# Attention and gated MLP on one core: the scores and values of two pairs of heads as one group of matmuls each

## The chip, the core and the metric

The kernel runs on one NeuronCore of a Trainium2 chip. Its engines are TensorE (PE, with its weight loads shown apart as PEld), VectorE (DVE), ScalarE (ACT), GpSimd (POOL) and SyncE (SP, which here only issues DMAs). The metric is the device time of one execution in microseconds, lower is better. Matmuls write to PSUM, which has eight banks of 512 fp32 values in each of 128 partitions; everything else works from SBUF.

## What is computed

Eight batches of 576 positions with 8 heads of 64 go through attention with a short causal window, and the concatenated heads through an MLP whose gate is a convolution over the sequence:

```python
scores = scale * np.matmul(q, k.transpose(0, 1, 3, 2))
rel = pos[:, None] - pos[None, :]
mask_plain = (rel >= 0) & (rel < 32)                          # heads 0 to 3
mask_dil = (rel >= 0) & (rel < 128) & (rel % 4 == 0)          # heads 4 to 7
attn = softmax(np.where(masks, scores, -1e9))
x = np.matmul(attn, v).transpose(0, 2, 1, 3).reshape(B, S, H * D)      # 8 x 576 x 512
h = np.maximum(x @ w_in, 0.0)                                 # 512 -> 1024
conv_out = sum of conv_w[k] * (h shifted by k - 1), k = 0, 1, 2
out = h * sigmoid(conv_out) @ w_out                           # 1024 -> 512
```

w_in, w_out and conv_w arrive as 64-bit floating-point numbers, as pairs of 32-bit words.

## The kernel before

**Attention.** A batch has four pairs of heads p = 0 to 3: two plain ones (kind 0) and two dilated ones (kind 1). `attention(b, p)` adds the tasks of one pair. A query block has 32 rows and sees 64 keys, so a head has 18 blocks; `scores()` (L250, matmul on L258) computes the 36 blocks of a pair with matmuls on 64x32 tiles of the array into the PSUM tile `att`, into nine slots of 64 columns: blocks 0 to 15 fill the two banks of the two heads, the leftovers 16 and 17 go to a third bank, on two of the four groups of 32 partitions for each head. In dilated pairs a leftover takes two matmuls. The softmax follows on DVE and ACT: scores plus mask out of `att` (L270, two additions), row maximum (L272), exponential, row sum, reciprocal (L292), product (L293), transposition in blocks of 32 into `pt` (L295). In batches 0 and 1 (`SLOTS`) the exponential is nine ACT instructions with their sums (L279); later it is one, with one more DVE pass ahead (L285) and one behind (L290). `values()` (L306) multiplies by `v` with matmuls on 32x64 tiles, into `att` again: 40 (plain) or 32 (dilated) in the main part, 8 or 16 for the leftovers. Its result is split into a rounded part `x..a` (ACT, L344) and the remainder `x..b`: in batches 0 and 1 (`HELPED`) by PE, which subtracts `x..a` in place with matmuls by minus one (L351, L354), and an ACT cast (L359); later by DVE (L361).

**The MLP.** `expert(b)`: the first layer computes 8 chunks of 128 columns in two halves of 288 positions. A half takes 12 matmuls 128x288 (L386): for each of the four pairs' `x`, high times high, high times low, low times high. ACT's ReLU writes `h` (L393). The gate of a chunk: a scaled copy (ACT, L404), two convolution taps (DVE, L398), sigmoid (ACT, L409), the product with `h` (DVE, L411), then high and low part into `g` (ACT L413, DVE L415). The second layer takes 24 matmuls of 512 columns (L431) for each 128 positions, 256 columns in batch 0; ACT copies them out (L441) and SP stores them.

**Weights.** The eight chunks of w_in and w_out are converted on the chip into a high and a low part by `weights()` (L495 to L510: two ACT and seven DVE instructions of 1024 columns).

**Order.** Nothing is issued as written. Each operation is a task with an engine, a guessed cost, a due time and the buffers it needs. `Planner.order()` imitates the engines with these costs and takes, among the tasks of an engine that could start within 0.25 us of the first, the one with the smallest due time; the `DUE` table holds the due times. The resulting order of each engine is the program. A task waits in the plan until a buffer of its pool is free. The pools that matter here: one `att` tile of four PSUM banks for scores and values alike, two `qk`, three `v`, three `s`, two `pt`, seven `x`, three `h`, three `c`, two `mm` and two `nn` banks for the two layers, two `out`.

## Time and profile before

| | |
|---|---|
| median of 3 runs | 533.38 us (532.96 to 534.69) |
| the profiled execution | 535.56 us, its span 533.8 us |
| L431, second layer, PE | 960 matmuls, 212.0 us |
| L386, first layer, PE | 1536 matmuls |
| L306, values, PE | 3072 matmuls, 44.7 us |
| L258, scores, PE | 2432 matmuls, 36.6 us |
| DVE, ACT busy | 397.3 us, 303.7 us |

The span is the time from the first to the last instruction of the program; the execution's own time is 1.8 us longer. The trace counts each fp32 matmul of the scores and values twice (1216 and 1536 in the program). A matmul's duration overlaps those of its neighbours, so what one costs is read from the distance of starts.

### The profile page before, as it was taken

The numbers are of one execution on the slowest core, as the hardware profiler recorded it, in microseconds if no ns is written. First come the engines' busy times: TensorE is split into PE (matmuls) and PEld (weight loads), VectorE is DVE, ScalarE is ACT, GpSimd is POOL, SyncE is SP. The second block draws the span as 40 slices with busy tenths as digits, with TensorE's granted clock in tenths as the row PEclk, the third lists the DMA queues.
The fourth block names the chain that finished last, engine by engine and source line by source line (L and its number), as shares of the span: only waits on it lengthen the run. The fifth ranks groups of instructions, "written<-read, shape, count | busy, mean of one in ns | idle before, by whom it ended". The sixth has DMA issues, their size and how long they took to land.

```text
span 533.8 us, 17819 instructions
## 1 busy us (share of the span) xinstructions
PE 505.9 (95%) x8048; PEld 449.4 (84%) x8048; DVE 397.3 (74%) x611; ACT 303.7 (57%) x660; POOL 1.0 (0%) x15
## 2 busy tenths in 40 slices
PE   3569999999999999999999999999999999999996
PEld 2459899998877998789977899789988899789985
DVE  5987999998986799859996569828997277607900
ACT  4975998638632587237742377517764386427710
POOL 0000000000000000000000000000000000000000
PEclk9999999999999999999999999999999999999999
DMA  8846721233145312451224401321313100110011
GB/s 301 297 164 210 241 60 31 80 127 101 43 170 163 97 32 79 154 182 59 83 67 149 148 33 48 121 96 53 104 47 119 52 2 1 59 42 1 0 50 50
DMA packets 16556, 52.24 MB, mean 98 GB/s; under 512 B 2016, under 2 KB 3168, under 8 KB 15456
## 3 DMA queue, kind: packets, MB, share of 16 engines
q1 hardware_dynamic: 16336, 51.02, 28.6%
q8 instruction: 63, 1.03, 0.8%
q14 instruction: 13, 0.11, 0.1%
q10 hardware_dynamic: 144, 0.08, 0.1%
HBM read 41.66 MB, written 9.44 MB: 96 GB/s over the span
## 4 chain that ended last, share of the span: by engine, by line
PE 80%; DVE 8%; ACT 7%; DMA 3%; issue 1%; ACTq 0%
PE nn L431 34%; PE mm L386 31%; PE att L306 8%; PE att L258 4%; ACT s L279 3%; PE nn L386 2%; DVE c L398 2%; PE att L351 1%; DMA qk<-in_qk_p_dram 1%; DVE t L501 1%; DVE wo L510 1%; ACT c L409 1%; DMA c<-in_mask_dram 1%; DVE c L411 1%; DVE g L415 1%
## 5 line engine op out<-in xcount | busy, mean ns | idle before, releaser
L431 PE MATMUL nn<-wo,g 128*128 128x512 f32 (+1 forms) x960 | 212.0, 375 | 0.0
L431 PEld LDWEIGHTS nn<-wo,g 128*128 128x128 f32 x960 | 163.4, 188 | 33.4
L398 DVE SCALAR_TENSOR_TENSOR c<-h,conv_sb,c 128x576 f32<-128x576 f32 x128 | 103.5, 816 | 32.8 <-ACT c L404 31.1
L393 ACT ACTIVATE h<-mm 128x288 f32<-128x288 f32 x120 | 48.5, 408 | 43.9 <-PE mm L386 40.8
L441 ACT COPY out<-nn 128x512 f32<-128x512 f32 (+1 forms) x40 | 21.7, 542 | 72.5 <-PE nn L431 45.1
L413 ACT CAST g<-c 128x576 fp32r<-128x576 f32 x64 | 42.4, 672 | 17.7 <-DVE c L411 15.7
L411 DVE TENSOR_TENSOR c<-c,h 128x576 f32<-128x576 f32 x64 | 47.9, 756 | 5.9 <-ACT c L409 5.4
L306 PEld LDWEIGHTS att<-pt,v 32*64 32x64 f32 x3072 | 41.2, 140 | 13.1 <-issue 8.5
L415 DVE TENSOR_TENSOR g<-c,g 128x576 fp32r<-128x576 f32 x64 | 47.6, 755 | 4.5 <-ACT g L413 3.4
L404 ACT ACTIVATE c<-h,conv_sb 128x576 f32<-128x576 f32 x64 | 49.4, 778 | 1.3
L386 PE MATMUL mm<-x1a,wi 128*128 128x288 f32 x176 | 49.7, 297 | 0.0
L258 PE MATMUL att<-qk 64*32 64x64 f32 x2432 | 36.6, 237 | 13.4 <-DMA qk<-in_qk_p_dram 5.3
L258 PEld LDWEIGHTS att<-qk 64*32 64x32 f32 x2432 | 30.4, 112 | 22.2 <-issue 7.7
L409 ACT ACTIVATE c<-c 128x576 f32<-128x576 f32 x64 | 43.2, 684 | 10.3 <-DVE c L398 9.4
L306 PE MATMUL att<-pt,v 32*64 32x64 f32 (+2 forms) x3072 | 44.7, 234 | 3.8 <-DVE s L270 1.3
L386 PE MATMUL mm<-x2a,wi 128*128 128x288 f32 x144 | 41.6, 304 | 1.3 <-ACT h L393 1.3
L386 PE MATMUL mm<-x0a,wi 128*128 128x288 f32 x144 | 40.6, 297 | 0.0
L270 DVE TENSOR_TENSOR s<-att,mask_sb 128x512 f32<-128x512 f32 x64 | 26.6, 450 | 16.3 <-PE att L258 16.2
L386 PE MATMUL mm<-x6a,wi 128*128 128x288 f32 x128 | 36.6, 301 | 0.8 <-ACT h L393 0.7
L386 PE MATMUL mm<-x5a,wi 128*128 128x288 f32 x128 | 36.2, 298 | 0.2 <-ACT h L393 0.2
L386 PE MATMUL mm<-x4a,wi 128*128 128x288 f32 x128 | 35.9, 295 | 0.0
L295 DVE STREAM_TRANSPOSE pt<-s 128x576 f32<-128x576 f32 x32 | 24.8, 776 | 11.9 <-PE att L306 10.9
(134 smaller groups left out, 808.7 us busy)
## 6 DMA issues: line engine op xcount, KB each, us to landing
qk<-in_qk_d_dram SPq DMA_DIRECT2D x16, 664.0 KB, 4.3
qk<-in_qk_p_dram SPq DMA_DIRECT2D x16, 592.0 KB, 4.1
out_dram<-out SPq DMA_DIRECT2D x28, 256.0 KB, 2.2
v<-in_v_d_dram SPq DMA_DIRECT2D x16, 384.0 KB, 3.1
v<-in_v_p_dram SPq DMA_DIRECT2D x16, 384.0 KB, 3.4
raw<-in_w_in_dram SPq DMA_DIRECT2D x4, 1024.0 KB, 6.6
raw<-in_w_out_dram SPq DMA_DIRECT2D x4, 1024.0 KB, 4.7
out_dram<-out SPq DMA_DIRECT2D x16, 128.0 KB, 2.4
```

What stands on the lines that cost most here:

```text
L258: nc.tensor.matmul(sc.t[quad * 32:quad * 32 + 32, slot // 4, slot % 4 * W:slot % 4 * W + W], q, k, start=i == 0, stop=i == len(parts) - 1, ...
L270: last = plan.add("DVE", cost, soft + 0.0, lambda i=i: nc.vector.tensor_tensor(out=two(flat())[i], in0=scored()[i], in1=two(masked)[i], op ...
L306: nc.tensor.matmul(tv.t[hd * 64:hd * 64 + 64, bank, o:o + n], v.t[quad * 32:quad * 32 + 32, block // 2, block % 2 * 64:block % 2 * 64 + 64 ...
L386: nc.tensor.matmul(ps.t[:, 0:HALF], wi[jw][fc // 2][:, fc % 2, k], x[k].t[jx][:, hf * HALF:hf * HALF + HALF], start=(k == 0 and i == 0), s ...
L393: relu.append(plan.add("ACT", 0.4, due + 1.6 * u + 1.6, lambda fc=fc, hf=hf, ps=ps: nc.scalar.activation(out=h[fc].t[:, 1 + hf * HALF:1 + ...
L398: nc.vector.scalar_tensor_tensor(out=c[fc].t, in0=h[fc].t[:, k:S + k], scalar=conv_sb[:, k, fc:fc + 1], in1=c[fc].t, op0=ALU.mult, op1=ALU ...
L404: t = plan.add("ACT", 0.777, d, lambda fc=fc: nc.scalar.activation(out=c[fc].t, in_=h[fc].t[:, 1:S + 1], func=AF.Copy, scale=conv_sb[:, 1, ...
L409: t = plan.add("ACT", 0.686, d + 1.0, lambda fc=fc: nc.scalar.activation(out=c[fc].t, in_=c[fc].t, func=AF.Sigmoid), [t], [c[fc]], "sigmoid")
L411: t = plan.add("DVE", 0.755, d + 1.5, lambda fc=fc: nc.vector.tensor_tensor(out=c[fc].t, in0=c[fc].t, in1=h[fc].t[:, 1:S + 1], op=ALU.mult ...
L413: hi = plan.add("ACT", 0.675, d + 2.0, lambda fc=fc: nc.scalar.copy(out=half(fc, 0), in_=c[fc].t), [t, *(done[fc] if odd else [])], [c[fc] ...
L415: lo = plan.add("DVE", 0.755, d + 2.5, lambda fc=fc: nc.vector.tensor_tensor(out=half(fc, 1), in0=c[fc].t, in1=half(fc, 0).bitcast(F32), o ...
L431: nc.tensor.matmul(ps.t[:, 0:n], g[k // 2].t[:, k % 2, jg, c0:c0 + 128], w.rearrange("p h c -> p (h c)") if hf is None else w[:, hf], star ...
```

## The change

- `attention(b, kind)` now handles both pairs of a kind. In batches 1 to 7 (`JOINED_S`, `JOINED_V` = 0xfffc) their scores are one task and their values one task. The joined scores need both pairs' `qk` and two `s`; the second pair's blocks lie 256 columns further in the same banks and its leftovers in the fourth bank. The joined values need both pairs' `v` and `pt` and two `x`; the second pair's result lies 160 columns further in the same four banks.
- The leftovers of a pair's second member are placed on the other two groups of partitions (`place`, and the host's layout of `v`), and the leftovers of the two pairs alternate.
- The pool `h` has nine buffers in place of three; the planner can give a task several buffers of one pool; some guessed costs and all due times are new; the space set aside for dynamic DMA is 1024.

```diff
+JOINED_S, JOINED_V = 0xfffc, 0xfffc
 DUE = {
-    "first": (72.60, 66.90, 228.40, 589.20, 119.60, 531.50, -87.70, 234.00),
+    "first": (161.60, -49.30, 126.20, 1200.50, 75.70, 1241.80, 240.10, 1169.20),
...
+        wanted = {}
         for b in t.uses:
             if b.t is None:
-                if not self.free[b.pool]:
+                n = wanted[b.pool] = wanted.get(b.pool, 0) + 1
+                if len(self.free[b.pool]) < n:
                     return None
-                at = max(at, min(self.free[b.pool])[0])
+                at = max(at, sorted(x[:2] for x in self.free[b.pool])[n - 1][0])
...
-    hs = slots("h", 3, [128, S + 2])
+    hs = slots("h", 9, [128, S + 2])
...
-        return 8, 2 * hd + n - 16
+        return 8, (2 * hd + n - 16 + 2 * (p % 2)) % 4
...
+    def scores(sc, pairs):
+        def one(o, n, hd):
+            slot, quad = place(o.p, hd, n)
+            c0, bank = (slot % 4 * W + 256 * o.first, slot // 4) if n < 16 else (0, 2 + o.first)
+            parts = queries(o.p, o.qk.t, hd, n)
+            for i, (q, k) in enumerate(parts):
+                nc.tensor.matmul(sc.t[quad * 32:quad * 32 + 32, bank, c0:c0 + W], q, k,
+                                 start=i == 0, stop=i == len(parts) - 1, skip_group_check=True)
+        for o in pairs:
+            for i in range(4):
+                for t in range(4):
+                    for hd in range(2):
+                        one(o, 4 * t + i, hd)
+        for n in (16, 17):
+            for hd in range(2):
+                for o in pairs:
+                    one(o, n, hd)
...
+        for kh in range(2):
+            for r in range(1 + kind):
+                for g, hd in turns[:4]:
+                    for o in pairs:
+                        c0, g2 = 512 + 32 * kh, g + 2 * (o.p % 2)
...
-            last = plan.add("ACT", 2.7, soft + 1.5, exps, [last], [s, m, z], "exp")
+            last = plan.add("ACT", 3.1, soft + 1.5, exps, [last], [s, m, z], "exp")
...
+        joined = lambda bits: [both] if bits >> (2 * b + kind) & 1 else [[o] for o in both]
+        for pairs in joined(JOINED_S):
+            sc = Buffer("att")
+            for i, o in enumerate(pairs):
+                o.first = i
+            last = plan.add("PE", (0.8, 0.92)[kind] if len(pairs) == 1 else (1.55, 1.75)[kind], SCORES[b][pairs[0].p],
+                            lambda sc=sc, pairs=pairs: scores(sc, pairs),
+                            [o.lq for o in pairs], [sc, *(x for o in pairs for x in (o.qk, o.s))], "S")
+            for o in pairs:
+                softmax(o, sc, last)
+        done = []
+        for pairs in joined(JOINED_V):
+            tv = Buffer("att")
+            for i, o in enumerate(pairs):
+                o.second = i
+            last = plan.add("PE", (1.05, 1.15)[kind] if len(pairs) == 1 else (1.9, 1.95)[kind], VALUES[b][pairs[0].p],
+                            lambda tv=tv, pairs=pairs: values(tv, pairs),
+                            [x for o in pairs for x in (o.lv, o.last)],
+                            [tv, *(x for o in pairs for x in (o.v, o.pt, o.x))], "V")
+            done += [split(o, tv, last) for o in pairs]
...
-            cost, base = (0.682, 0) if hf is None else (0.36, hf * n)
+            cost, base = (0.697, 0) if hf is None else (0.345, hf * n)
...
-    nc = bacc.Bacc("TRN2", target_bir_lowering=False, num_devices=1)
+    nc = bacc.Bacc("TRN2", target_bir_lowering=False, num_devices=1, dynamic_dma_scratch_size=1024)
```

Three places show what it does to the order. The first is PE in the third batch. Before, the values of a pair (L306, out of `att`, from `pt` and `v`) are a visit of their own between second-layer matmuls (L431):

```order
L306 MATMUL att_124<-pt_94,v_83 64x64 x24
L306 MATMUL att_124<-pt_94,v_83 64x32 x8
L306 MATMUL att_124<-pt_94,v_83 64x16 x16
L431 MATMUL nn_128<-wo_73,g_112 128x512 x2
L431 MATMUL nn_128<-wo_75,g_112 128x512
L431 MATMUL nn_127<-wo_72,g_109 128x512 x2
L431 MATMUL nn_127<-wo_74,g_109 128x512
L431 MATMUL nn_127<-wo_72,g_109 128x512 x2
L431 MATMUL nn_127<-wo_74,g_109 128x512
L306 MATMUL att_124<-pt_94,v_82 64x64 x24
L306 MATMUL att_124<-pt_94,v_82 64x32 x8
L306 MATMUL att_124<-pt_94,v_82 64x16 x16
```

After, the values (L277) of two pairs follow each other, from both `pt` buffers, between second-layer matmuls (L478):

```order
L478 MATMUL nn_134<-wo_72,g_109 128x512 x2
L478 MATMUL nn_134<-wo_74,g_109 128x512
L277 MATMUL att_130<-pt_93,v_82 64x32 x8
L277 MATMUL att_130<-pt_93,v_82 64x64 x24
L277 MATMUL att_130<-pt_93,v_82 64x32 x8
L277 MATMUL att_130<-pt_94,v_81 64x32 x8
L277 MATMUL att_130<-pt_94,v_81 64x64 x24
L277 MATMUL att_130<-pt_94,v_81 64x32 x8
L277 MATMUL att_130<-pt_93,v_82 64x32
L277 MATMUL att_130<-pt_94,v_81 64x32
```

Two visits of 48 matmuls have become one of 96, whose leftovers alternate between the pairs; 28 visits of scores and 28 of values in batches 1 to 7 have become 14 and 14.

The second is DVE at the end of the second batch's softmax. Before, the two last pairs of that batch end in two transpositions (L295), with a convolution tap (L398) between, behind the fourth conversion of weights:

```order
L508 TENSOR_SCALAR raw_122<-t_123 128x1024
L510 SCALAR_TENSOR_TENSOR wi_71<-raw_122 128x1024
L292 RECIPROCAL z_92<-z_92 128x9
L293 TENSOR_TENSOR s_86<-s_86,z_92 128x9x64
L295 STREAM_TRANSPOSE pt_93<-s_86 128x576
L292 RECIPROCAL z_91<-z_91 128x9
L293 TENSOR_TENSOR s_85<-s_85,z_91 128x9x64
L398 SCALAR_TENSOR_TENSOR c_116<-h_113,conv_sb,c_116 128x576
L295 STREAM_TRANSPOSE pt_93<-s_85 128x576
L398 SCALAR_TENSOR_TENSOR c_116<-h_113,conv_sb,c_116 128x576
L398 SCALAR_TENSOR_TENSOR c_117<-h_114,conv_sb,c_117 128x576 x2
```

After, the last pair of one joined group (`s_86`) and the two of the other are transposed (L334) with a piece of a conversion (L555, L557: the fifth, the fourth of w_in) between:

```order
L332 TENSOR_TENSOR s_86<-s_86,z_92 128x9x64
L334 STREAM_TRANSPOSE pt_94<-s_86 128x576
L555 TENSOR_SCALAR raw_127<-t_129 128x1024
L331 RECIPROCAL z_90<-z_90 128x9
L332 TENSOR_TENSOR s_84<-s_84,z_90 128x9x64
L557 SCALAR_TENSOR_TENSOR wi_68<-raw_127 128x1024
L334 STREAM_TRANSPOSE pt_93<-s_84 128x576
L445 SCALAR_TENSOR_TENSOR c_122<-h_113,conv_sb,c_122 128x576
L331 RECIPROCAL z_91<-z_91 128x9
L332 TENSOR_TENSOR s_85<-s_85,z_91 128x9x64
L334 STREAM_TRANSPOSE pt_94<-s_85 128x576
```

The conversion of one chunk of w_out has moved ahead of the last transposition of that batch, and the first batch's convolution taps have not moved past it.

The third is DVE in the third batch, where `att` is drained. Before, the subtraction for one pair (L361, the tile `x3b`) stands behind one transposition, and the next pair's scores are added to the mask soon after:

```order
L295 STREAM_TRANSPOSE pt_93<-s_86 128x576
L361 TENSOR_TENSOR x3b<-att_124,x3a 128x512
L361 TENSOR_TENSOR x3b<-att_124,x3a 128x64
L290 TENSOR_REDUCE z_90<-s_84 128x9
L292 RECIPROCAL z_90<-z_90 128x9
L293 TENSOR_TENSOR s_84<-s_84,z_90 128x9x64
L270 TENSOR_TENSOR s_85<-att_124,mask_sb 128x8x64
L270 TENSOR_TENSOR s_85<-att_124,mask_sb 128x64
L272 TENSOR_REDUCE m_88<-s_85 128x9
L285 TENSOR_TENSOR s_85<-s_85,m_88 128x9x64
```

After, two pairs are transposed, and then four subtractions (L375) drain two joined visits:

```order
L332 TENSOR_TENSOR s_85<-s_85,z_91 128x9x64
L332 TENSOR_TENSOR s_86<-s_86,z_92 128x9x64
L334 STREAM_TRANSPOSE pt_93<-s_85 128x576
L334 STREAM_TRANSPOSE pt_94<-s_86 128x576
L375 TENSOR_TENSOR x1b<-att_130,x1a 128x512
L375 TENSOR_TENSOR x1b<-att_130,x1a 128x64
L375 TENSOR_TENSOR x2b<-att_130,x2a 128x512
L375 TENSOR_TENSOR x2b<-att_130,x2a 128x64
L375 TENSOR_TENSOR x3b<-att_130,x3a 128x512
L375 TENSOR_TENSOR x3b<-att_130,x3a 128x64
L375 TENSOR_TENSOR x4b<-att_130,x4a 128x512
L375 TENSOR_TENSOR x4b<-att_130,x4a 128x64
```

A visit's `att` is now given back after two pairs' work.

## What is predicted

> **What bounds the kernel now.** The page comes first: the busy line, the TensorE slices and the granted clock. Then the stages, as windows cut where the first layer of the second batch begins (84) and where the second layer of the second batch has begun (137).
>
> ```profile
> span 533.8 us, 17819 instructions
> PE 505.9 (95%) x8048; PEld 449.4 (84%) x8048; DVE 397.3 (74%) x611; ACT 303.7 (57%) x660; POOL 1.0 (0%) x15
> PE   3569999999999999999999999999999999999996
> PEclk9999999999999999999999999999999999999999
> 5.00:45.00 40.00, 24.52 (x796) 22.05 (x796) 34.15 (x60) 28.54 (x124) 0.00 (x0) 1.00 0.73 265
> 45.00:84.00 39.00, 37.03 (x825) 34.91 (x824) 35.51 (x52) 34.39 (x111) 0.00 (x0) 1.00 0.45 144
> 84.00:137.00 53.00, 52.25 (x543) 50.39 (x542) 49.88 (x65) 36.52 (x63) 0.00 (x0) 1.00 0.26 87
> 137.00:330.00 193.00, 192.71 (x3486) 168.37 (x3485) 155.59 (x251) 101.71 (x188) 0.00 (x0) 1.00 0.31 99
> 330.00:530.00 200.00, 199.37 (x2429) 173.70 (x2410) 122.15 (x186) 100.91 (x177) 0.00 (x0) 1.00 0.17 55
> ```
>
> The columns of a window are its length, then PE, PEld, DVE, ACT and POOL busy. From 137 on PE is idle for 0.29 + 0.63 us in 393: the time is the sum of what PE does. Before 84 it is not: DVE, with 34.15 of 40 and 35.51 of 39, and ACT carry the softmax of the first batches and the conversion of the weights. From 84 to 137 both are full (PE 52.25, DVE 49.88 of 53).
>
> So I price PE's work. The chain gives undisturbed runs of the two layers, the timeline the visits of attention between them (start, length to the modelled end, matmuls; the trace shows two for each fp32 matmul of the program):
>
> ```profile
> 489.63 12.81 PE mm L386 x96
> 502.44 27.32 PE nn L431 x117
> 338.92 0.97 PE L258 MATMUL att<-qk 64*32 64x64 f32 x72
> 339.82 6.56 PE L431 MATMUL nn<-wo,g 128*128 128x512 f32 x27
> 346.31 1.26 PE L306 MATMUL att<-pt,v 32*64 32x32 f32 x96
> 347.50 1.20 PE L431 MATMUL nn<-wo,g 128*128 128x512 f32 x4
> 358.24 1.06 PE att L258 x65
> 408.40 1.36 PE L306 MATMUL att<-pt,v 32*64 32x64 f32 x96
> 409.69 4.47 PE L431 MATMUL nn<-wo,g 128*128 128x512 f32 x18
> 414.09 1.36 PE L306 MATMUL att<-pt,v 32*64 32x64 f32 x96
> ```
>
> A first-layer matmul takes 12.81/96 = 0.133 us, a second-layer one 27.32/117 = 0.2335. From start to start, plain scores take 339.82 - 338.92 = 0.90, dilated ones 1.06, plain values 347.50 - 346.31 = 1.19, dilated ones 409.69 - 408.40 = 1.29. The 27 matmuls after the scores take 6.49, 0.19 more than 27 x 0.2335; the 18 after the values 4.40, 0.20 more. So each visit costs 0.19 beside its own time: 1.09, 1.25, 1.38 and 1.48, and a batch with two of each 10.4 us.
>
> **The joined visits.** Joining two pairs removes one surcharge of 0.19 and the first group's start and end; the second pair's matmuls are added at the pace of the group's inside. Matmuls of one line in a window (those in flight at its start are counted, so the difference of two counts):
>
> ```profile
> 339.33:339.34 0.01, 0.01 (x16) 1.00 0.00 0
> 339.33:339.53 0.20, 0.20 (x38) 1.00 0.00 0
> 346.64:346.65 0.01, 0.01 (x20) 1.00 0.00 0
> 346.64:346.99 0.35, 0.35 (x52) 1.00 0.00 0
> ```
>
> Scores: 22 in 0.19 us, 8.6 ns each. Values: 32 in 0.34, 10.6 each. The leftover blocks (the last two of 18) are slower: dilated scores have 8 more of them than plain ones and take 0.16 longer, 20 ns each, since one pair's leftovers use half of the row groups at a time. The joined form interleaves the two pairs' leftovers on opposite halves, so the second pair's leftovers add between nothing and 20 ns each. Main and leftover matmuls in the trace: plain scores 64 + 8, dilated 64 + 16, plain values 80 + 16, dilated 64 + 32. A joined visit, surcharge included:
> - plain scores 0.90 + 0.55 + (0 to 0.16) + 0.19 = 1.64 to 1.80, saves 0.38 to 0.54 against 2 x 1.09;
> - dilated scores 1.06 + 0.55 + (0 to 0.32) + 0.19 = 1.80 to 2.12, saves 0.38 to 0.70;
> - plain values 1.19 + 0.85 + (0 to 0.32) + 0.19 = 2.23 to 2.55, saves 0.21 to 0.53;
> - dilated values 1.29 + 0.68 + (0 to 0.64) + 0.19 = 2.16 to 2.80, saves 0.16 to 0.80.
>
> Together 1.13 to 2.57 a batch. I take 2.0, nearer the upper end: two streams of 20 ns that interleave give 10, the pace of the main part. The Trainium skill, "TensorE: Matmul & The Clock Gate", section "Wait — 56ns, not 53.3ns?", says that starts of matmuls never lie closer than about 25 ns; by that rule 72 more matmuls would cost 1.8 us, more than a visit of their own does now, and nothing would be saved. The 22 starts in 0.19 us above speak against it for matmuls on small tiles.
>
> Seven batches are joined, but the second one's attention lies before 84, where PE isn't the bound; I count six: **12.0 us** (6.8 to 15.4).
>
> **The start.** The same state in both programs is PE's first matmul of the second batch's first layer: all attention of two batches and the whole first layer of batch one are done. Now it is at 83.64. After it the bound is DVE again until the last gate of the second batch at 144.04:
>
> ```profile
> 83.64 0.38 PE L386 MATMUL mm<-x6a,wi 128*128 128x288 f32 x1
> 15.20 0.78 DVE L270 TENSOR_TENSOR s<-att,mask_sb 128x512 f32<-128x512 f32 x2
> 18.42 0.78 DVE L270 TENSOR_TENSOR s<-att,mask_sb 128x512 f32<-128x512 f32 x2
> 106.20 0.69 DVE L504 TENSOR_SCALAR raw<-raw 128x1024 int32<-128x1024 int32 x1
> 112.39 0.69 DVE L504 TENSOR_SCALAR raw<-raw 128x1024 int32<-128x1024 int32 x1
> 7.49 0.81 DVE L270 TENSOR_TENSOR s<-att,mask_sb 128x512 f32<-128x512 f32 x2
> 143.28 0.76 DVE L415 TENSOR_TENSOR g<-c,g 128x576 fp32r<-128x576 f32 x1
> ```
>
> A pair's softmax keeps DVE for 18.42 - 15.20 = 3.22 us, a weight chunk's conversion for 112.39 - 106.20 = 6.19. In the new order, ahead of the transposition that the last joined values of batch two need, DVE has eight softmaxes, five conversions, one convolution tap (0.8) and what precedes 7.49: 25.8 + 31.0 + 0.8 + 7.5 = 65.1 us. To this comes idle time. It is 5.85 + 3.49 = 9.3 us in the first two windows now; with 7 to 10, that transposition ends at 72 to 75. Behind it PE has the joined values (2.3), 6 matmuls (0.8), the 12 subtractions, and ACT's casts (0.7 a pair) on both sides: 6 to 9 us. The state is reached at 78 to 84, say 82. Nine h buffers don't move that point: they let PE do first-layer work of batches one and two while the gates, which free them, are late. After it DVE has up to the last gate the same work as now except some 2.5 us of batch three's softmax, which comes later. PE can thus be 1 to 4 us earlier at 137, unless it waits for a joined V: there both pairs' softmax must be done, the second up to 3.2 us after the first. I take **1.5 us** (-1 to 4).
>
> **New waits.** There is one att tile for scores and values. It is held until both pairs are drained, so the next visit waits longer:
>
> ```profile
> 157.33 0.70 ACT L344 CAST x3a<-att 128x64 fp32r<-128x64 f32 x2 [1.96 <-PE att L306]
> 158.07 0.82 DVE L361 TENSOR_TENSOR x3b<-att,x3a 128x512 fp32r<-128x512 f32 x2
> 157.33 0.78 DVE L295 STREAM_TRANSPOSE pt<-s 128x576 f32<-128x576 f32 x1 [0.20 <-PE att L306]
> qk<-in_qk_d_dram SPq DMA_DIRECT2D x16, 664.0 KB, 4.3
> ```
>
> After values: two casts of 0.70 and a subtraction of 0.82, 2.2 us if DVE is free, 3.7 behind two transpositions. The order leaves 12 second-layer matmuls (2.8 us) there in the third batch and 15 (3.5) at two later places, 21 to 27 elsewhere. After scores: two pairs' additions (0.78 a pair, above), 1.6 us, against 2.1 (9 matmuls) at the tightest. The queries of two pairs must have landed (4.3 us each) where 15 matmuls, a joined V and 15 matmuls, 9.2 us, lie between two scores. Five places can wait, for 0 to 1 us each. Behind such a visit stand the matmuls of both layers on PE, and behind these ACT's copies and the stores. I take **-1.5 us** (0 to -5). The waits that go (0.9 us from 137 on) are within this.
>
> **At nothing.** Twelve more memsets on POOL stand ahead of the identity's last step, which is at 1.27 now, while ACT takes the identity at 5.59, after the first convolution weights; uncovered, a memset of 0.10 each makes 1.2 us. The smaller scratch for dynamic DMA: the transfers are in a hardware queue, and I see no use of it. The block placement in the host's layout changes no size. The planner's corrected costs only set the order: 0.697 for three second-layer matmuls agrees with 3 x 0.2335, and 3.1 for a pair's exponentials with the last of these rows, so the planned order should miss fewer waits:
>
> ```profile
> 1.27 0.29 POOL masks.py:199 TENSOR_SCALAR_AFFINE_SELECT pt<-pt 128x128 f32<-128x128 f32 x1
> 5.59 0.29 ACT L518 ACTIVATE minus<-pt 128x128 fp32r<-128x128 f32 x1
> q1 hardware_dynamic: 16336, 51.02, 28.6%
> 9.37 3.10 ACT s L279 x18
> ```
>
> **Sum.** 12.0 + 1.5 - 1.5 = 12.0 us. The profiled execution took 535.56 (its span of 533.8 and 1.8 around it) and would take 523.6. The median of the runs is 533.38, so I predict **521.4 us**.
>
> **Rivals.**
> - *Joined groups run hardly better than two single ones* (the lower ends, and 3 us of waits): 6.8 - 3 = 3.8, so 529.6. The slow leftovers speak for it, the interleaved halves against.
> - *The start is lost*: the joined values of batch two wait for both softmaxes behind conversions, the state comes 3.4 us after 83.64: 12.0 - 3.4 - 1.5 = 7.1, so 526.3. DVE's order with a conversion between the two softmaxes speaks for it.
> - *PE falls back to its slow pace.* Six first-layer matmuls took 1.63 us at 43.71 and nine 1.40 at 46.40, though the granted clock is 1.0 in both:
>
> ```profile
> 43.71 1.63 PE nn L386 x6
> 46.40 1.40 PE mm L386 x9
> ```
>
>   Nine at the later pace take 0.155 each, six at the earlier 0.27. A long wait for a joined V could bring the slow pace back; twice 1.8 us gives 525.0. The Trainium skill, same page, section "Part 1: The HAM clock gate (the "warmup" mystery)", says that PE runs at half its clock after a window of about 3.4 us without work. The two paces agree with that; the granted clock in the profile does not show it.
> - *The start wins more*, and the lower PE load passes on whole: gain 17, so 516.4.
> - *Slower*: the single att tile. If each of the twelve later joined values waits for the second pair's softmax (on DVE the 3.22 us above and two more passes of about 0.8, 4.8 a pair, behind gates), the gain of 13.5 is gone from 1.1 us a wait on; at 1.8 it is 533.4 - 13.5 + 21.6 = 541.5. Against it: by the order 10 to 20 us of PE work lie between a visit's scores and its values, where two softmaxes take 9.6, and DVE is busy for 122 of 200 us after 330.
>
> That the change doesn't do what it says is excluded by the order, which shows 14 joined visits of each kind.
>
> **Chances.** Forecast 0.58, joined groups no better 0.10, start lost 0.10, slow pace 0.07, start wins more 0.10, slower 0.05. The bounds of the terms give 514.0 to 532.6; the range that leaves out 2 in 10 is 515 to 529. Within 0.3% (1.6 us, what a measurement can tell) only the worst of the first rival falls: 0.04. Faster 0.91, slower 0.05.
>
> **What would show it.** Joined scores at 1.5 to 1.9 us and joined values at 2.0 to 2.6 from start to start, with one surcharge each, prove the first term; 3 us for values would refute it. The first matmul of batch two at 78 to 84, and PE's idle time after 137 below 3 us, prove the others. Values that PE waits for at many places, or a first-layer pace of 0.27 after 50, would make the prediction wrong.

## The result, and the profile after

| kernel | median | runs |
|---|---|---|
| changed | 555.98 us | 548.28, 553.92, 558.04, 559.23 |
| before, the same chip | 533.95 us | 532.96 to 534.69, 4 runs |

By the medians the changed kernel is slower by 22 us, where 12 us faster was predicted (521.4, range 515 to 529). The ratio is 1.032, with a 95% interval of 1.023 to 1.042; here and below, a ratio leaves out runs more than 1.5% above the fastest of their kernel (here 558.04 and 559.23; the other two are 14.3 and 20.0 us slower than before), while a median is over all of them. The four runs have a mean granted clock of 0.959 to 0.976, the profile before 1.0; the lower clock comes with the change, as will be seen.

The page of the changed kernel, its profiled execution of 558.04 us, to which the account below belongs:

```profile
span 556.2 us, 17757 instructions
...
PE 509.3 (92%) x8048; PEld 455.7 (82%) x8048; DVE 394.7 (71%) x611; ACT 301.5 (54%) x658; POOL 1.4 (0%) x27
...
PEclk9999999999977999899998989999999899799999
...
q8 instruction: 63, 1.03, 0.8%
...
L277 PE MATMUL att<-pt,v 32*64 32x64 f32 (+2 forms) x3072 | 41.2, 236 | 24.1 <-issue 19.7
```

PE is idle for 47 us of the span; before it was 28. The values matmuls (L277 now) wait for 24.1 us in all, and 19.7 of these are put down to "issue": nothing that the profile shows was missing. The granted clock, full in all forty slices before, has seven slices below 0.9 behind the first quarter. The waits of PE from 137 us on, by what they wait for (sum, times, longest), are these three rows and no others:

```profile
PE att L277 <- issue: 16.6, 7, 4.4
PE att L255 <- issue: 1.7, 1, 1.7
PE mm L433 <- issue: 1.7, 1, 1.7
```

Where they lie is seen in the timeline (start, length, count of matmuls, and in brackets the idle time before the row):

```profile
82.56 0.38 PE L433 MATMUL mm<-x4a,wi 128*128 128x288 f32 x1
...
150.69 1.89 PE L255 MATMUL att<-qk 64*32 64x64 f32 x160
152.51 2.36 PE L478 MATMUL nn<-wo,g 128*128 128x512 f32 x9
154.80 1.64 PE L277 MATMUL att<-pt,v 32*64 32x32 f32 x136
159.72 1.17 PE L277 MATMUL att<-pt,v 32*64 32x64 f32 x56 [3.28 <-issue]
...
169.77 2.02 PE L277 MATMUL att<-pt,v 32*64 32x64 f32 x172
173.62 0.61 PE L277 MATMUL att<-pt,v 32*64 32x16 f32 x20 [1.82 <-issue]
...
192.86 1.66 PE L255 MATMUL att<-qk 64*32 64x64 f32 x144
194.45 0.40 PE L433 MATMUL mm<-x1a,wi 128*128 128x288 f32 x1
...
220.17 2.17 PE L277 MATMUL att<-pt,v 32*64 32x64 f32 x191
224.16 0.23 PE L277 MATMUL att<-pt,v 32*64 32x16 f32 x1 [1.82 <-issue]
...
230.93 2.24 PE L277 MATMUL att<-pt,v 32*64 32x32 f32 x192
233.09 3.30 PE L478 MATMUL nn<-wo,g 128*128 128x512 f32 x13
...
426.20 1.97 PE L277 MATMUL att<-pt,v 32*64 32x32 f32 x171
432.61 0.64 PE L277 MATMUL att<-pt,v 32*64 32x32 f32 x21 [4.44 <-issue]
```

A joined visit that does not stop costs 1.59 us (194.45 - 192.86, plain scores), 1.82 (152.51 - 150.69, dilated scores) and 2.16 (233.09 - 230.93, values). That is what was predicted. But some visits stop in the middle: the values visit of 154.80 after 136 of its 192 matmuls, for 3.28 us, that of 169.77 after 172, that of 426.20 after 171 for 4.44 us. The nine waits last 1.65 us or more each, 20.0 us in all.

**What they have in common.** Visits are counted among the joined ones, in PE's order. The matmul that has to wait has so many matmuls of the program ahead of it (the trace records all 8048):

| visit | values 3 | values 4 | values 5 | scores 9 | values 9 | behind scores 11 | values 11 | values 12 | values 14 |
|---|---|---|---|---|---|---|---|---|---|
| matmul | 2521 | 2776 | 3543 | 4692 | 5330 | 5970 | 6482 | 6865 | 7631 |
| modulo 128 | 89 | 88 | 87 | 84 | 82 | 82 | 82 | 81 | 79 |
| wait, us | 3.28 | 1.82 | 1.82 | 1.71 | 1.65 | 1.69 | 1.65 | 4.44 | 1.98 |

They are 128 apart, or a multiple of it, less one now and then. A matmul has a weight load, so 128 matmuls are 256 instructions; a few waits on semaphores that are instructions of their own make the small drift. The trace has 38 more instructions on PE (35 on semaphores, 3 drains), and counted with them all nine waiting matmuls have 192 or 193 instructions, modulo 256, ahead of them. And 8048 + 8048 + 38 instructions in the 63 packets of queue q8, "instruction", are 256 to a packet, 1.03 MB / 63 = 16 KB. So PE gets its program in blocks of 256 instructions, and these waits stand at block boundaries. This is the view of the DMA traffic of 169 to 173 us, in slots of 0.1 us:

```profile
GB/s 430 389 205 21 0 0 0 0 0 0 0 0 0 0 0 0 0 0 0 0 0 0 164 0 0 0 0 0 0 0 0 0 0 0 0 0 0 0 0 0
...
q8 instruction: 1, 0.02, 1.4%
```

From 169.4 on one block is moved, at 171.2, and nothing else; the values visit stops at 171.8 and goes on at 173.62. It had passed the boundary before, 128 matmuls earlier, at about 169.77 + 44 x 0.0115 = 170.3: from there to the end of the wait it takes 3.3 us. In the fifth values visit (220.17) the same sum gives 220.9 to 224.16, 3.3 us again. The packets of q8 show the same in all nine waits: the transfer of a block starts 0.7 to 1.3 us behind the boundary before (2.45 and 3.61 in the two long waits, values 3 and 12), and the waiting matmul starts 2.35 to 2.43 us after that (2.77 in values 14). In none of the profiles of this case does PE run a block less than 2.18 us after its transfer starts.

The reading (theory A): PE holds two blocks; when it begins the second, the next is asked for; some 3.3 us later it can run. A joined visit uses up 128 matmuls in 1.4 us and waits for the other 1.9. A visit of 96 matmuls, as before, cannot hold two boundaries; of the twelve joined values visits after 137 us, seven wait inside, by where they happen to stand in the program. Two boundaries in a visit are not enough, though: scores visits 7 and 10 and values visit 13 hold two, the first of them 13, 6 and 5 matmuls from the visit's start, and lose 0, 0 and 0.2 us. There the block's transfer starts 0.8 to 1.3 us before the matmul at the first boundary runs. That PE's queue reads ahead, further where the slower matmuls of the layers stand in front, would explain it; no run here shows it.

**And the clock.** These are windows of 3.41 us (busy time of PE, and "PEclk"), laid on the steps of the granted clock, each time one with the next behind it:

```profile
core 0: us, PE busy (x) PEld busy (x) DVE busy (x) ACT busy (x) POOL busy (x), PEclk, DMA share, GB/s
156.02:159.44 3.42, 0.42 (x38) 0.28 (x27) 3.34 (x8) 1.35 (x2) 0.00 (x0) 1.00 0.50 200
159.44:162.85 3.41, 3.13 (x61) 2.68 (x62) 2.62 (x5) 1.31 (x4) 0.00 (x0) 0.50 0.28 90
...
169.68:173.09 3.41, 2.12 (x173) 1.93 (x173) 0.00 (x0) 0.00 (x0) 0.00 (x0) 1.00 0.02 5
173.09:176.51 3.42, 2.89 (x26) 2.37 (x26) 0.74 (x2) 1.40 (x4) 0.00 (x0) 0.50 0.31 105
...
415.45:418.86 3.41, 2.19 (x45) 1.89 (x46) 1.55 (x3) 1.31 (x4) 0.00 (x0) 1.00 0.21 40
418.86:422.27 3.41, 3.41 (x149) 2.73 (x148) 3.04 (x7) 0.00 (x0) 0.00 (x0) 1.00 0.54 203
```

The granted clock is halved for 3.41 or 6.83 us directly behind a window in which PE was busy for 0.42 or 2.12 us; behind one with 2.19 it stays. In the profiles of the changed kernel and of nine of the experiments below (e1, e4 to e10, e12), from 40 us on, all 21 windows at the full clock in which PE was busy for 1.77 us or less were followed by half the clock; between 1.8 and 2.25 us both happened, and above that it fell three times, all between 74 and 84 us. It is no strict rule: in the profile of e3_shifted, below, four such windows were followed by half the clock and one of 1.65 us, at 478.82, was not, and ahead of 40 us the clock of the changed kernel stayed full behind a window with 1.11 us (22.90). So a wait of 1.8 us costs its own time, and, where it falls into one window, mostly 1.7 us more for each window that is then halved. The waits of 1.69 us at 375.43 and 1.65 us at 416.67 happened to lie so that they cost nothing more. Behind 137 us, and ahead of the end, the clock is halved for 34.1 us.

**The sum.** From PE's first matmul of the second batch's first layer, the state that the prediction used, it is 473.6 us to the end (556.2 - 82.56), and was 450.2 (533.8 - 83.64): 23.4 more. The joins take 12 away (as predicted, and as the filled version below measures), the waits add 20.0, and the 15.4 that are left over are put down to the halved clock: 34.1 us at half pace lose 17 if PE has work all the time. The 15.4 are a remainder and were not measured by themselves.

### The profile page after: what moved, and what is told of

It reads as the page before. It is cut to its first block, busy times and chain, and to the rows that moved or that the text cites. A ratio compares the mean times of both kernels' runs of the same rounds, so it can differ in the third digit from the quotient of the medians.

```text
span 556.2 us, 17757 instructions
## 1 busy us (share of the span) xinstructions
PE 509.3 (92%) x8048; PEld 455.7 (82%) x8048; DVE 394.7 (71%) x611; ACT 301.5 (54%) x658; POOL 1.4 (0%) x27
## 3 DMA queue, kind: packets, MB, share of 16 engines
q8 instruction: 63, 1.03, 0.8%
## 4 chain that ended last, share of the span: by engine, by line
PE 85%; ACT 6%; issue 5%; DVE 3%; DMA 1%; ACTq 0%; DVEq 0%
PE nn L478 39%; PE mm L433 33%; PE att L277 6%; PE att L255 5%; ACT s L318 2%; PE nn L433 1%; PE att L365 1%; DMA c<-in_mask_dram 1%; DVE s L309 1%; ACT t L542 1%; DVE raw L553 0%; DVE m L311 0%; ACT h L440 0%; ACT wo L550 0%; DVE s L332 0%
## 5 line engine op out<-in xcount | busy, mean ns | idle before, releaser
L478 PE MATMUL nn<-wo,g 128*128 128x512 f32 (+1 forms) x960 | 220.4, 388 | 0.1
L478 PEld LDWEIGHTS nn<-wo,g 128*128 128x128 f32 x960 | 173.6, 197 | 36.9 <-ACT out L488 0.3
L277 PE MATMUL att<-pt,v 32*64 32x64 f32 (+2 forms) x3072 | 41.2, 236 | 24.1 <-issue 19.7
L277 PEld LDWEIGHTS att<-pt,v 32*64 32x64 f32 x3072 | 38.0, 141 | 28.4 <-issue 22.4
L433 PE MATMUL mm<-x4a,wi 128*128 128x288 f32 x160 | 45.5, 299 | 0.3 <-ACT h L440 0.3
L255 PE MATMUL att<-qk 64*32 64x64 f32 x2432 | 31.7, 236 | 12.7 <-DMA qk<-in_qk_p_dram 4.9
L255 PEld LDWEIGHTS att<-qk 64*32 64x32 f32 x2432 | 28.0, 111 | 18.0 <-issue 5.2
L433 PE MATMUL mm<-x1a,wi 128*128 128x288 f32 x144 | 41.2, 302 | 0.0
L433 PE MATMUL mm<-x3a,wi 128*128 128x288 f32 x144 | 41.1, 301 | 0.0
L309 DVE TENSOR_TENSOR s<-att,mask_sb 128x512 f32<-128x512 f32 (+1 forms) x64 | 26.5, 447 | 17.0 <-PE att L255 17.0
L334 DVE STREAM_TRANSPOSE pt<-s 128x576 f32<-128x576 f32 x32 | 24.7, 775 | 15.9 <-PE att L277 15.1
```

The costliest lines, as they stand in the source:

```text
L255: nc.tensor.matmul(sc.t[quad * 32:quad * 32 + 32, bank, c0:c0 + W], q, k, start=i == 0, stop=i == len(parts) - 1, skip_group_check=True)
L277: nc.tensor.matmul(tv.t[hd * 64:hd * 64 + 64, bank, at:at + n], o.v.t[quad * 32:quad * 32 + 32, block // 2, block % 2 * 64:block % 2 * 64 ...
L309: last = plan.add("DVE", cost, soft + 0.0, lambda i=i: nc.vector.tensor_tensor(out=two(flat())[i], in0=scored()[i], in1=two(masked)[i], op ...
L433: nc.tensor.matmul(ps.t[:, 0:HALF], wi[jw][fc // 2][:, fc % 2, k], x[k].t[jx][:, hf * HALF:hf * HALF + HALF], start=(k == 0 and i == 0), s ...
L478: nc.tensor.matmul(ps.t[:, 0:n], g[k // 2].t[:, k % 2, jg, c0:c0 + 128], w.rearrange("p h c -> p (h c)") if hf is None else w[:, hf], star ...
```

## The experiments

The rivals to theory A: **B**, the smaller scratch for dynamic DMA makes transfers or instruction blocks late; **C**, the new order, the single att tile or the nine h buffers cost the time; **D**, the clock throttles by itself, as an answer to the joined visits' small matmuls.

### The halves apart

```diff
-        for t in plan.order():
-            t.run()
+        while left:
+            t = left.pop(0)
+            t.run()                      # the first pair alone
+            if t.rest:
+                for _ in range(APART):   # up to 4 tasks of the layers
+                    x = next((x for x in left if x.engine == "PE"), None)
...
+                    x.run()
+                t.rest()                 # the second pair
```

> The changed program in its own order and with all its buffers, but each joined visit is cut into its two pairs, and the next 6 to 12 matmuls of the first or second layer go between them (the last values visit stays joined). Theory A (PE runs out of instructions: they come in blocks of 256, and a joined values visit of 384 can use up a block in 1.4 us, faster than the next one arrives): the waits inside the visits go, except about 2 us in the last one; the granted clock is 1.0 nearly throughout; PE pays the switches again (about 12 us), so 532 to 537 us. Rival C (the new order, the single att tile's longer hold or the nine h buffers cost the time): these are all as before, so 550 us or more.

Measured: 578.96 us, ratio 1.080 (1.077 to 1.083), slower still than the changed kernel. The waits named "issue" fell from 23.5 to 6.2 us, but others came:

```profile
PE att L275 <- DVE s L307: 10.3, 7, 2.3
PE att L258 <- DVE x3b L373: 5.7, 2, 3.0
PE att L275 <- issue: 5.6, 5, 1.4
```

The matmuls between the halves were taken from behind the visit, where they had covered the time in which DVE and ACT empty the att tile. Without this cover the next visit waits for the mask addition (L307) and the subtraction (L373). So the experiment changed two things. It speaks for A in the waits inside the visits and decides nothing about C; the later ones do.

### The scratch alone

```diff
-    nc = bacc.Bacc("TRN2", target_bir_lowering=False, num_devices=1)
+    nc = bacc.Bacc("TRN2", target_bir_lowering=False, num_devices=1, dynamic_dma_scratch_size=1024)
```

> The kernel before with nothing changed but the smaller scratch for dynamic DMA. Theory A: no difference, 532.5 to 534.5 us, no waits inside the visits. Rival B (the smaller scratch makes transfers and instruction loads late): waits of 1 us or more inside visits appear, and the time rises to 540 or more.

Measured: 535.11 us beside 535.65, ratio 0.9995 (0.9975 to 1.0015), and after 137 us PE has no wait over 0.6 us. This program has no joined visit that could wait for a block, but the blocks come as promptly as before: their transfers start 0.67 us (median, after 137 us) behind a boundary, with the larger scratch 0.70. Rival B is out.

### The same program, 200 instructions further on

```diff
+    for _ in range(50):
+        nc.tensor.matmul(nns[0][0][0:32, 0:64], ident[0:64, 0:32], ident[0:64, 0:64], start=True, stop=True,
+                         skip_group_check=True)
     with tc.manual_schedule():
```

> The changed program with 50 small extra FP32 matmuls (200 instructions) ahead of everything on PE, while it waits for the first queries. They compute nothing that is used; every later instruction stands 200 places further. Theory A: a wait occurs only where a second block boundary falls into a joined visit, so the places move. In the changed kernel the waits over 1 us lie, after 137 us, in joined values visits 3, 4, 5, 9, 11, 12 and 14 (counted in PE's order) and in scores visit 9. Here they should lie in values visits 3, 10, 11, 13, about 1 us in scores visit 6, and just behind values visit 14; none in values 4, 5, 9 and 12 nor in scores 9. Waits sum to about 10 to 14 us instead of 23.5, halved clock 10 instead of 34 us: 540 to 548 us. Rivals C and D (the order or the buffers; a clock that throttles by itself): the same places and 553 to 559 us.

Measured: 557.16 us, ratio 1.039 (1.036 to 1.042). The waits after 137 us are 10.7 us, at five places: values visits 3, 11 and 13, scores visit 5 and just behind values visit 14. So most places moved as said, with two misses: scores visit 6 ran through, and visit 5 waited 1.2 us at its only boundary (the one before lies 4 matmuls ahead of the visit); and values visit 10, whose first boundary lies 11 matmuls from its start, ran through in 2.14 us. The time did not follow, because the extra matmuls were not cheap:

```profile
7.67 10.55 PE L588 MATMUL nn<-pt 64*32 64x64 f32 x97
```

They all write one place of one tile, take 0.109 us each, and came behind the first pair's scores: 10 us of the start. The next version puts them into the first scores visit, over eight places in turn.

```diff
+        for j in range(ahead.pop() if ahead else 0):     # 50, once
+            one(pairs[0], j // 2 % 4 * 4, j % 2)
         for o in pairs:
             for i in range(4):
```

> As e3_shifted, but its 50 extra matmuls stand in the very first scores visit and write to eight places in turn, so that they cost 1 us of the start and not 10. Theory A: the same places wait as in e3 (values visits 3, 11, 13, scores visit 6, and just behind values visit 14; about 11 us in all), none in values visits 4, 5, 9, 12 and scores 9, and the time is 541 to 549 us, some 10 less than the changed kernel. Rivals C and D: 553 to 559 us.

Measured: 547.5 us, ratio 1.019 (1.013 to 1.025), the time as expected. Its timeline at visits that can be compared with those above:

```profile
162.31 1.99 PE L281 MATMUL att<-pt,v 32*64 32x32 f32 x164
167.56 0.45 PE L281 MATMUL att<-pt,v 32*64 32x32 f32 x28 [3.25 <-issue]
...
175.99 2.19 PE L281 MATMUL att<-pt,v 32*64 32x64 f32 x192
178.11 3.07 PE L482 MATMUL nn<-wo,g 128*128 128x512 f32 x12
...
405.79 2.11 PE L281 MATMUL att<-pt,v 32*64 32x64 f32 x182
410.28 0.31 PE L281 MATMUL att<-pt,v 32*64 32x16 f32 x10 [2.38 <-issue]
```

Values visit 3 now stops after 164 matmuls instead of 136, values visit 11 after 182 instead of 154: 28 later in both, since 100 matmuls further in the program is 28 short of a block. Values visit 4 stopped after 172 and now runs through in 2.12 us. All waits over 0.6 us after 137: 11.7 us (two small ones, 0.8 and 0.9, were not foreseen, and of the scores visits 5 waits again and not 6). Order, tiles and buffers are those of the changed kernel: rivals C and D don't move a wait by 28 matmuls.

### Filling, so that no visit holds two boundaries far inside

A few of a visit's first matmuls are repeated (the results are the same), so that later visits stand elsewhere in their blocks. In the first version a repeat wrote the same place each time, in the second eight places in turn:

```diff
+PADS = (0, 0, 0, 2, 20, 0, 0, 0, 0, 8, 16, 0, 0, 3, 0, 0, 0, 0, 4, 0, 0, 21, 0, 8, 0, 0, 0, 0)
...
+        for j in range(next(pads) if len(pairs) == 2 else 0):
+            one(pairs[0], j // 2 % 4 * 4, j % 2)
         for o in pairs:
             for i in range(4):
...
+        for j in range(next(pads) if len(pairs) == 2 else 0):
+            t, hd = turns[j % 8]
+            begun.clear()
+            pv(pairs[0], (t + 2 * hd) % 4, hd, t, hd, ...)
```

> The changed program with 3 extra matmuls ahead of everything and a few repeats of a joined visit's first matmul (82 in ten of the visits, about 1.7 us in all; results are the same), chosen so that no joined visit holds two block boundaries far enough inside. Nothing else is different: visits stay joined, same order, same buffers. Theory A: no wait over 1 us inside the visits, granted clock 1.0, and the joined visits keep their gain: 521 to 529 us, faster than before. Rivals C and D: 553 to 560 us.

Measured: 537.96 us, ratio 1.0005 (0.997 to 1.004): 18 us less than the changed kernel, but not the 521 to 529 expected. The profiled execution has a span of 530.4, the clock at 1.0, and 3.2 us of waits over 0.6 after 137 (20.0 in the changed kernel). What it lost is in the repeats:

```profile
386.51 4.01 PE L257 MATMUL att<-qk 64*32 64x64 f32 x186
390.45 1.90 PE L486 MATMUL nn<-wo,g 128*128 128x512 f32 x7
```

The visit of 144 + 42 matmuls takes 3.94 us, where 144 take 1.59. The trace shows two matmuls for each of the 21 repeats: 0.11 us a repeat, and for 82 of them 9 us.

> As e4_filled, same number of repeats in the same visits and so the same block boundaries, but the repeats go round over eight places of the att tile instead of writing one place again and again (and the first 3 stand in the first scores visit). In e4 a repeat cost about 0.11 us, a run of 42 matmuls 2.35 us. If that is what e4 lost (82 repeats, some 9 us, where 0.022 each or 1.8 was meant), the profiled span is 521 to 526 us where the granted clock stays at 1.0, with no wait over 1 us inside the visits but one near the end, behind two loads of queries. If joined visits lose those 8 us in another way (rival C), it stays at 530.

Measured: 533.17 us (525.38 to 535.48), ratio 0.988 (0.979 to 0.996); the profiled span is 523.6. The same visit:

```profile
381.59 2.08 PE L259 MATMUL att<-qk 64*32 64x64 f32 x186
383.60 2.60 PE L491 MATMUL nn<-wo,g 128*128 128x512 f32 x10
...
400.63 1.55 PE L285 MATMUL att<-pt,v 32*64 32x32 f32 x129
404.82 1.08 PE L285 MATMUL att<-pt,v 32*64 32x64 f32 x63 [2.64 <-issue]
```

It takes 2.01 us: the repeats now cost 0.02 each. One long wait is left, in values visit 12. After 137 us four visits still hold two boundaries, the first within eight matmuls of the start (values 6, 7, 11 and 12). Three of them lose 0.5 us or less, and there the block's transfer starts 1.0 to 1.2 us before the first boundary's matmul runs; in visit 12 it starts 1.7 us behind it. The same kernel, profiled again and then measured for its interval:

> The kernel of e5_filled_apart once more, unchanged, for the profile of another execution. By theory A its waits lie at the same places, above all the one near 402 us (2.86 us in e5), and what differs in time from e5's 523.6 is the halved clock behind them and the start.

> The kernel of e5_filled_apart once more, for its interval: the executions so far took 525.4, 527.9, 532.7, 533.7 and 535.5 us. Theory A: faster than the kernel before by 0.5 to 1.5%; a few executions near 525 and more near 533, by the clock that they were granted.

Measured: 527.85 us for one execution, with the same wait at the same matmul (2.4 us); then 530.57 us (529.21 to 531.94, 5 runs), ratio 0.9905 (0.9887 to 0.9922). This version beats the kernel before by 1% and the changed one by some 25 us, with all of the change in it: the same order, the joins, the buffers. Rival C is out. From the state above to the end e9_filled_again takes 445.1 us; less 4.0 of waits, 1.8 of repeats and 2.5 of halved clock, 436.8. For e5_filled_apart the same is 444.8 - 4.5 - 1.8 - 1.7 = 436.8, and for the kernel before 450.2 - 1.3 of waits = 448.9: the joins are worth 12 us in both.

### Filling without dense work

```diff
         for t in order:
             t.run()
+            for _ in range(after.get(t, 0)):             # up to 6 behind three matmuls of the layers
+                nc.tensor.nop(hint="fill", nofuse=True)
```

> The changed program with 873 instructions that do nothing on PE, two behind each matmul of the two layers ahead of 18 of the joined visits, so that each visit's block boundaries fall where they do no harm; nothing dense is added and nothing else is different. Theory A: no wait over 1 us inside a joined visit, granted clock 1.0 but for chance; if the no-ops fit beside the 0.15 and 0.23 us matmuls, 519 to 527 us; if each takes PE 0.05 us of its own, some 40 us more, but the visits still without waits. Rivals C and D: the waits inside the visits stay at about 20 us.

Measured: 534.81 us, ratio 0.997 (0.994 to 1.001); the profiled clock is 0.999. After 137 us the values visits have no wait over 1.0 us any more, but two scores visits with 30 no-ops close ahead of them do, one of them:

```profile
402.00 1.35 PE L256 MATMUL att<-qk 64*32 64x64 f32 x113
405.16 0.46 PE L256 MATMUL att<-qk 64*32 64x64 f32 x31 [1.81 <-issue]
```

Here A was wrong in part: this visit holds one boundary, and it waits. A no-op shortens the time that a block lasts, and takes PE's instruction queue time of its own (0.06 us, below); which of the two it was isn't told apart. The block's transfer starts 1.8 us behind the boundary before, which lies ahead of the visit, and PE goes on 2.9 us later. The third way, both fillings mixed and more of them, did no better:

> The changed program with 174 repeats in the visits (eight places in turn) and 170 no-ops ahead of them, so that every joined visit but one has its block boundary at least some ten matmuls from the places that make it wait, also where an instruction block comes 2 us late behind loads of queries. Theory A with late blocks as the cause of e5's last wait and of part of its slower executions: no wait over 1 us inside the visits; the filling costs 174 x 0.022 + 170 x 0.01 = 5.5 us, so a span of 522 to 527 where the clock is 1.0, and a median of 525 to 531, with less spread than e5 (525 to 535). If the slower executions have another cause, the median stays at 532 to 537.

Measured: 535.53 us, ratio 1.002 (1.000 to 1.005). It removed the wait of values visit 12, but after 137 us scores visits waited four times, up to 1.4 us and 4.6 in all, after 115 matmuls, at their only boundary, again behind no-ops or repeats. The reading, which was not tried by itself: the filling, too, uses up blocks quickly.

### Why two waits are twice as long

```diff
-            ... lambda o=o, n=n: nc.sync.dma_start(
+            ... lambda o=o, n=n: b > 1 or nc.sync.dma_start(
```

> The changed program without the loads of queries, keys and values from the third batch on (the tiles keep older data, so the output is not the reference's). Theory A with late blocks: in the changed kernel two waits were far longer than the others, 3.49 us in values visit 3 and 4.66 in values visit 12, where the instruction block came behind loads of queries; the rest were 1.8 to 2.2. Without those loads no wait is over 2.2 us, and those two are 1.7 to 2.1. The others stay, since their blocks came undelayed (boundaries move by up to ten matmuls, so one or two visits may change sides). If the loads play no part, the two long waits stay at 3 us or more.

Measured (one execution): 548.45 us. The two long waits of the changed kernel, 3.28 and 4.44 us, are now:

```profile
155.49 1.64 PE L277 MATMUL att<-pt,v 32*64 32x32 f32 x137
159.21 0.81 PE L277 MATMUL att<-pt,v 32*64 32x64 f32 x55 [2.08 <-issue]
...
420.03 2.10 PE L277 MATMUL att<-pt,v 32*64 32x32 f32 x180
424.22 0.33 PE L277 MATMUL att<-pt,v 32*64 32x32 f32 x12 [2.09 <-issue]
```

No wait is longer than 2.1 us, and after 137 us no block's transfer starts more than 1.3 us behind its boundary, where it was 2.45 and 3.61. So the blocks come late where they stand behind loads of queries, which a joined visit sets off in pairs (two of 664 KB each at 152.57 and at 422.59 in the changed kernel; the loads of values are left out here as well). And a by-product: without loads there are no instructions that wait for them, and all ten waits over 0.6 us stand at a matmul whose number, counted as in the table above, is 90 modulo 128 (2522, 2778, 3546, 4698, 5082, 5338, 6490, 6874, 7258, 7642). The drift of the table above is gone.

### The clock without joined visits

```diff
+            for _ in range(240 if t in pauses else 0):   # behind eight second-layer tasks, in the kernel before
+                nc.tensor.nop(hint="pause", nofuse=True)
```

> The kernel before, without any joined visit, but with PE held up eight times by 240 no-ops behind a second-layer matmul. Theory A says that the granted clock is halved for 3.41 us because PE was idle for more than about a third of the 3.41 us window before, whatever the cause: where a pause leaves a window busy for less than 0.5 to 0.6 of it, the next window has 0.5; where it is split over two windows, 1.0. Pauses of 2 us or more should give 3 to 8 such windows. Rival D (it is the small matmuls of the joined visits that the clock reacts to): 1.0 throughout, as in the kernel before. If the pauses come out under 1.3 us, neither is tested.

Measured: 673.45 us. The pauses came out at 13.3 to 16.4 us, 0.056 to 0.068 a no-op. One of the eight:

```profile
269.60:273.20 3.60, 0.23 (x1) 0.00 (x0) 3.10 (x7) 2.90 (x4) 0.00 (x0) 1.00 0.00 0
273.20:286.20 13.00, 0.07 (x1) 0.10 (x1) 3.77 (x6) 0.00 (x0) 0.00 (x0) 0.50 0.00 0
286.20:290.20 4.00, 4.00 (x10) 3.14 (x11) 0.00 (x0) 0.00 (x0) 0.00 (x0) 0.50 0.02 4
290.20:293.60 3.40, 3.40 (x16) 2.61 (x14) 0.00 (x0) 1.01 (x2) 0.00 (x0) 0.99 0.33 77
```

The clock is full for one window of the pause, half for the rest of it and for 4.0 us of full work behind it, and then full again; so at all eight, and nowhere else. In a kernel without a joined visit, idleness alone halves the clock: D in its form "it is the small matmuls" is out. That a wait of 1.8 us in one window is enough was not tried by itself; it is read from the windows of the changed kernel and of the experiments.

## Why the prediction was wrong

**What bounds the kernel** was right: after 84 us, PE's work. **The joined visits** were right: 1.59, 1.82 and 2.12 to 2.16 us where nothing waits, with the surcharge of 0.19 (not measured again) a saving of 0.40, 0.49, 0.45 and 0.65 for the four visits, 2.0 us a batch as predicted. That the 12.0 us are really there is shown by the filled version (12 us in two executions). **The start** came out as said, the state at 82.56, predicted 78 to 84, say 82, with a gain of 1.1 of the 1.5 us, but partly by luck: the transposition ended at 72.05 (72 to 75 expected), and the state came 10.5 us behind it instead of 6 to 9, because PE began the joined values only at 76.52, behind matmuls of the first layer. **The new waits** at the att tile, for which 1.5 us were taken off, did not come: after 137 us PE waits for no engine and no load. **At nothing** was right for the scratch (0.9995), which was tried; the memsets and the host's layout were not tried alone.

**The step that failed** is in "The joined visits": that a joined visit always runs on at the pace of a single visit's inside. Its price of 12.0 us holds for a visit that does not stop. The sum has no term for how fast PE gets its instructions; it was put at nothing, without a reason. But 192 small matmuls with their weight loads are 384 instructions in 2.1 us, and PE's program arrives in blocks of 256, which in these waits could run 3.2 to 3.7 us after the block before was entered, and 4.8 and 6.0 us behind loads. The missing term is 20.0 us of waits and, behind them, 15.4 us put down to the halved clock: 35 us against the 12 saved.

The views of before had its parts: 63 packets in a queue named "instruction", 16,096 matmuls and weight loads, and a pace of 10.6 ns inside a values visit, at which 128 last 1.4 us. What did not stand out was the 3.3 us, since no visit of the kernel before held two boundaries and none of its waits after 137 us exceeded 0.2 us. This queue was read as background. The Trainium skill, page "Runtime: NRT & Kernel Launch", section "🔬 Instruction fetch mechanics", says that each engine's program is fetched in 16 KiB blocks of 256 instructions by a DMA queue of its own, the next while the present one runs, and that crossing a block is mostly hidden. The runs agree on the block. Of the 46 boundaries after 137 us 37 show no wait in the trace of the changed kernel, so "mostly hidden" holds by count, but the other nine cost 1.65 to 4.44 us each; and where the page gives PE room for 2048 instructions, the waits fit room for two blocks.

Two of the rivals were near. "PE falls back to its slow pace" named the slower clock, but with a wait for a joined V as its cause and two cases of 1.8 us; it was seven stretches, and the cause was another. "Slower", by the single att tile, named a wait of 1.8 us at each of twelve joined values visits: seven waited, five of them for 1.65 to 1.98 us, but the size was right by chance and the mechanism wrong. The Trainium skill, page "TensorE: Matmul & The Clock Gate", section "Part 1: The HAM clock gate (the "warmup" mystery)", says that the clock is halved after an idle window of about 3.4 us, in windows that run freely. The steps of 3.41 us agree; but the window at 169.68 was not idle, PE worked in it for 2.12 us.

What stays open: executions of one and the same filled kernel lie between 525 and 536 us with mean granted clocks of 0.982 to 0.997. Their three profiles show halved windows behind the wait in values visit 12 in two of them and near the start in another; what decides this from run to run was not found. Nor was it found how far PE's queue reads ahead, and so which visits with a boundary near their start wait and which do not.

## What to carry to other kernels

Where small matmuls are put together into longer dense stretches, count instructions, not only time: weight loads count, an FP32 matmul of the scores or values here counts four (two matmuls and two weight loads in the trace), and a stretch that passes two boundaries of 256 instructions within some 3 us can wait for its program, unless the first lies at its very start. The queue "instruction" in the profile gives the blocks; a wait for "issue" in the middle of a group whose matmul numbers agree modulo 128 is the sign. Such a wait can then cost about its length once more through the clock, so read the granted clock of the window behind it.

## What the hardware showed that I had not expected

- PE's program comes in blocks of 256 instructions. A block's transfer starts 0.7 to 1.3 us after PE has passed the boundary before (in the waits of the changed kernel), and PE runs the block 2.35 to 2.77 us later, in no profile less than 2.18. Where two loads of 664 KB were under way, the transfer started 2.45 and 3.61 us behind the boundary, and the waits were 3.28 and 4.44 us; without the loads they were 2.08 and 2.09.
- Matmuls that write one place again and again took 0.056 us each (2.35 us for 42 in e4_filled) or 0.109 (10.55 us for 97 in e3_shifted, at the start), over eight places in turn 0.010 (0.42 us for 42).
- A no-op takes PE's instruction queue 0.056 to 0.068 us (13.3 to 16.4 us for 240). Up to six behind three matmuls of 0.13 to 0.23 us are mostly hidden: the 873 of e7_no_ops cost some 3 us from the state to the end (440.0 against 436.8 us in e5_filled_apart, with waits, repeats and halved clock taken off).
- The granted clock moves in steps of 3.41 us, and half a window of work does not hold it for sure: in ten profiles, from 40 us on, it fell behind all 21 windows with up to 1.77 us of work in 3.41, between 1.8 and 2.25 sometimes; one window of 1.65 us in another profile was not followed by a fall.
